# Moving a router's set-up arithmetic and one-hot tables from VectorE to GpSimd, and its blank output rows behind the set-up

## The chip, the cores and the metric

The kernel runs on one core of a Trainium2 chip. A core has TensorE (PE: matmuls and transposes), VectorE (DVE), ScalarE (ACT) and GpSimd (POOL), each of which takes its instructions in the order of the program, and SyncE (SP), whose queue starts most of the transfers, also in order. The engines wait for each other by semaphores. The metric is the device time of one execution in microseconds; lower is better.

## The reference

Three layers follow each other. Thresholded attention over 4 batches, 8 heads, 576 positions and 64 columns a head; then a mixture of 8 experts, of which each token takes the one with the largest logit; then a dense pair of layers over all 2304 tokens.

```python
scores = scale * np.matmul(q, k.transpose(0, 1, 3, 2))
thresh = np.max(scores, axis=-1, keepdims=True) - tau
scores = np.where(scores >= thresh, scores, -1e9)
attn = softmax(scores); x = attn @ v               # heads side by side: 2304 x 512
logits = x @ w_gate + modality_bias[modality_id]   # 2304 x 8
e_idx = np.argmax(logits, axis=1)
gate_w = softmax(logits)[np.arange(N), e_idx]
for e in range(E):                                 # 8 experts, 512 -> 1024 -> 512
    mask = e_idx == e
    y[mask] = gate_w[mask, None] * (np.maximum(x[mask] @ w1[e], 0) @ w2[e])
h = y @ w_in                                       # 512 -> 2048
return (h * sigmoid(1.702 * h)) @ w_out            # 2048 -> 512
```

## The kernel before

**Attention.** `Attention.run` goes through 72 iterations of two units; a unit is 128 rows of queries of one head against all keys, and nine units (`UPP`) make a pair of heads. TensorE computes the scores (`qk`, L234), VectorE takes the maximum (L245), ScalarE the exponential (L251), VectorE masks and sums (L275), TensorE transposes (L302) and multiplies by V (L348), ScalarE copies. GpSimd splits the next pairs' operands into high and low parts (`split`, L143 to L145; the last of the three buffers of `kA` and `kB` must be free for it) and scales finished rows (`row_items`, L386, L391), which SP writes to a buffer in DRAM, `x_dram` (L397).

**The side list.** Everything that doesn't belong to attention waits in a list, `side`. Each iteration takes one entry from it (`sides`; in the last 18 iterations up to eight, at five places). A `None` uses up a turn. At the start it holds seven `None`, then `gate_setup` (L102), the entries of `att.extra` (`blank_row` fills a tile on GpSimd, and ten `blank_rows` write it to the ten tiles of `y_rest` in DRAM, L1048 to L1052), and then the router's `setup_items`. Counted by iterations from 0, `gate_setup` is at 7, the blank rows at 8 to 18, and the set-up at 19 to 25. The order of instructions on each engine, and in SP's queue, is fixed by these lists when the program is built.

**The router.** `setup_items` (L543) loads the modality of each token (`mi`) and the biases (`bb`), makes row numbers and constants, and from them `idp` (the two digits of each token's number), `tri`, `rev`, `before`, `pages` and the bias of every token. After each batch `gate_items` finds the expert of each token. `assign` then gives every token a place in the experts' slots: assignment A after three batches (15 columns of 128 tokens, two slots), assignment B after the fourth (20 columns, all others). A token's place has two digits. `low` makes a one-hot table `OL` of the lower digit, 128 wide for each column of tokens, `high` one of the upper digit (`R`), `values` multiplies this by the token's number, and `sum_up` (L864) sums the products on TensorE; `lists` (L872 to L880) makes the indices for the gathers of it.

The order of these entries is at the end of `assign`:

```python
return [
    None, ranks, pages, starts, limits, slots, inside, counted, places, digits, high,
    lambda: (low(0, 5), values(0)), lambda: (low(5, 10), values(1)), lambda: low(10, n), gate,
    *[None] * (1 if first else NBW), lambda: sum_up(0, n), lists,
    ...
]
```

`gate`, behind the tables, ends with a copy on GpSimd (L670) and two writes by SP (L674) of each token's gate weight to `x_dram`.

**Experts and the last layer.** Seven slots of up to 512 tokens follow, two of assignment A and five of B. GpSimd gathers a slot's rows, TensorE transposes them (L929), and each slot takes eight steps of two matmul groups (L945, L967). SP loads an expert's weights in quarters (`ra` L1175, `rb` L1178); ScalarE rounds each (`ah`, `bh`, L1185) and VectorE takes the remainder (`al`, `bl`, L1186). Assignment B's arithmetic runs beside the steps of slot 0, and the weights of slot 1 are loaded behind it in SP's queue. Weights of the last layer are converted in between (L1089 to L1105). The last layer then runs over the tokens in blocks.

Of the kernel before, what the change touches and what calls it, by code (L numbers as in the profile page):

```python
# [14 lines left out]
ALU = mybir.AluOpType  # L15
# [6 lines left out]
NE = 8  # L22
# [3 lines left out]
PJ = 9  # L26
# [6 lines left out]
NS0 = 7  # L33
# [14 lines left out]
class Attention:  # L48
# [355 lines left out]
    def run(self):  # L404
        nc = self.nc
        NU = NPAIR * UPP
        self.load_first()
        self.load(1)
        rest = self.first()
        self.load_v(0)  # L410
        self.load_v(1)
        self.load(2)
        self.poolq = []
        self.avq, self.rowq, self.side = avq, rowq, side = [], [], []
        side += [None] * NS0 + [self.gate_setup, *self.extra] + self.router.setup_items(self.setup)
        it = done = 0
        while done < NU:
            last = it >= IT_LAST
            us = [u for u in (2 * it, 2 * it + 1) if u < NU]
            ts = [u for u in (2 * it - 2, 2 * it - 1) if 0 <= u < NU]  # L420
            starts = [u // UPP for u in us if u % UPP == 0]
            for p in starts:
                if p + 3 < NPAIR:
                    self.load(p + 3)
                if p + 2 < NPAIR:
                    self.load_v(p + 2)
                for n in range(1 if p == 0 else p + 2, min(p + 3, NPAIR)):
                    self.operands(n)
                    self.poolq += [lambda n=n, i=i: self.split(n, i, NPC) for i in range(NPC)]
            copies = []  # L430
            for i in range(2):
                if i < len(us):
                    self.qk(us[i])
                if i < len(ts):
                    copies += self.trans(ts[i])
                if i == 0 and not last:
                    n = AV1[it % 9]
                    while n and avq:
                        avq.pop(0)()
                        n -= 1  # L440
            for i in range(2):
                for c in range(2):
                    if CO[c] == 2 * i and c < len(copies):
                        copies[c]()
                if i < len(us):
                    self.max(us[i])
                    self.exp(us[i])
                for c in range(2):
                    if CO[c] == 2 * i + 1 and c < len(copies):
                        copies[c]()  # L450
                if last:
                    self.sides(SD[i], False)
            while rest:
                rest.pop(0)()
            for i, u in enumerate(us):
                self.mask(u)
                if last:
                    self.sides(SD[i + 2], False)
            n = AVL[it - IT_LAST] if last else AV[it % 9]
            while n and avq:  # L460
                avq.pop(0)()
                n -= 1
            for u in ts:
                self.trans_tails(u)
            n = ROWL[it - IT_LAST] if last else ROW[it % 9]
            while n and rowq:
                rowq.pop(0)()
                n -= 1
            n = 1
            while n and self.poolq:  # L470
                self.poolq.pop(0)()
                n -= 1
            self.sides(SD[4] if last else SN)
            for u in ts:
                done = u + 1
                p, w = divmod(u, UPP)
                if w == UPP - 1:
                    avq += self.av_items(p)
                    if p % 2:
                        avq.append(lambda b=p // HP, hh=p % HP // 2: rowq.extend(self.row_items(b, hh)))  # L480
            it += 1
# [33 lines left out]
PG = 512  # L515
# [7 lines left out]
class Router:  # L523
# [19 lines left out]
    def setup_items(self, tmp_pool):  # L543
        nc, c = self.nc, self.c
        T = lambda shape, name, dt=F32: c.tile(shape, dt, name=name)
        W = lambda shape, name, dt=F32: tmp_pool.tile(shape, dt, name=name)
        mi = W([64, B, PJ, 2], "mi", I32)
        bb = W([128, 2, NE], "bb")
        midf = W([128, B, 5], "midf")
        self.bias = T([128, NCOL, NE], "bias")  # L550
        tmp = W([128, NCOL, NE], "tmpb")
        nmid = W([128, NCOL], "nmid")
# [3 lines left out]
        pf = W([128, 1], "pf")  # L556
        ia = W([128, B, 5], "ia", I32)
        ib = W([128, B, 5], "ib", I32)
        i2 = W([128, 2, NCOL], "i2", I32)
# [12 lines left out]
        flat = midf.rearrange("p b c -> p (b c)")  # L572
        wide = lambda a: a.broadcast_to([128, NCOL, NE])
# [26 lines left out]
            nc.vector.tensor_scalar(i2[:, 1], iaf, 63, None, op0=ALU.bitwise_and)  # L600

        def tables():
            nc.vector.tensor_copy(self.idp, i2)
            nc.vector.tensor_scalar(self.tri, self.iota, pf[:, 0:1], None, op0=ALU.is_gt)
            nc.vector.tensor_scalar(self.rev, self.iota[:, 0:NE], -1.0, float(NE), op0=ALU.mult, op1=ALU.add)

        def order():
            e = self.iota[:, 0:NE]
            nc.vector.tensor_tensor(
                self.before, e.unsqueeze(2).broadcast_to([128, NE, NE]), e.unsqueeze(1).broadcast_to([128, NE, NE]),  # L610
                op=ALU.is_gt)
            nc.vector.tensor_scalar_mul(self.pages, e, float(PG))

        def modality():
            nc.vector.tensor_copy(midf[0:64], mi[:, :, 0:PJ:2, 0])
            nc.vector.tensor_copy(midf[64:128, :, 0:4], mi[:, :, 1:PJ:2, 0])
            nc.vector.tensor_scalar(nmid, flat, -1.0, 1.0, op0=ALU.mult, op1=ALU.add)

        def bias():
            nc.vector.tensor_mul(self.bias, wide(flat.unsqueeze(2)), wide(bb[:, 1:2, :]))  # L620
            nc.vector.tensor_mul(tmp, wide(nmid.unsqueeze(2)), wide(bb[:, 0:1, :]))
            nc.vector.tensor_add(self.bias, self.bias, tmp)

        return [loads, ids, parts, tables, order, modality, bias]

    def gate_items(self, b, lgt):
        nc, wk = self.nc, self.c
# [64 lines left out]
    def assign(self, ph, gate):  # L692
        nc, wk = self.nc, self.wk[ph]
        first = ph == "A"
# [9 lines left out]
        plf = T([128, 2, n], "plf")  # L704
        OL = T([128, n, 128], "OL", BF16)
# [136 lines left out]
            yield  # L842

        def low(c0, c1):
            nc.vector.tensor_tensor(
                OL[:, c0:c1], self.iota.unsqueeze(1).broadcast_to([128, c1 - c0, 128]),
                plf[:, 1, c0:c1].unsqueeze(2).broadcast_to([128, c1 - c0, 128]), op=ALU.is_equal,
            )

        def high():  # L850
            nc.vector.tensor_tensor(
# [2 lines left out]
            )  # L854

        def values(i):
            eng = nc.vector if i and first else nc.gpsimd
            eng.tensor_mul(R[:, :, i, :], R[:, :, 1, :], self.idp[:, i, 0:n].unsqueeze(2).broadcast_to([128, n, nh]))

        def sum_up(c0, c1):  # L860
# [24 lines left out]
        def compact():  # L885
# [12 lines left out]
# [4 lines that stand above are left out]
            *([] if first else [None] * 12 + [gaps, compact, None, bounds]),  # L902
# [578 lines left out]
```

## Time and profile before

| | |
|---|---|
| median of 3 runs | 985.03 us (983.91 to 985.19) |
| profiled execution | 986.93 us, span from first to last instruction 985.2 us |
| TensorE | 933.6 us busy (95%), granted clock 0.984 of full on average |
| VectorE | 556.5 us busy (56%) |
| ScalarE | 448.2 us busy (45%) |
| GpSimd | 236.2 us busy (24%) |

Attention takes the first 310 us or so, the experts run to about 600 us, the last layer to the end. The shares are averages over these stages, which have different limits; a stage has to be read by itself, from its own stretch of the timeline. A row of the timeline gives start, duration, engine, line and operation, and in square brackets how long the engine was idle before it and what it waited for. GpSimd's durations include time in which it waits for its port to the memory.

### The profile page before, as it was taken

The page shows a single profiled execution, that of the slowest core. Times are in us where ns is not written, and L with a number is a line of the kernel's source. Part 1 is how long each engine was busy: PE and PEld are TensorE (multiplying, and loading weights), DVE is VectorE, ACT ScalarE, POOL GpSimd, SP SyncE. Part 2 cuts the span into 40 slices and gives each one's busy share as a digit, 9 for nine tenths or more (in the row PEclk, how much of TensorE's full clock was granted, in tenths as well). Part 3 has the DMA queues.
Part 4 walks back from the last instruction along what each step waited for, and adds up shares of the span by engine and source line. Part 5 has one row for each costly group of instructions (what it writes and reads, how often), then busy time and mean ns, then how long its engine had stood idle before and what let it go on. Part 6 is the DMA issues. An engine that isn't in the chain of part 4 may idle for free. (4 is left out here: it accounts for less than half of the span.)

```text
span 985.2 us, 13988 instructions
## 1 busy us (share of the span) xinstructions
PE 933.6 (95%) x5009; PEld 751.8 (76%) x5009; DVE 556.5 (56%) x1194; ACT 448.2 (45%) x803; POOL 236.2 (24%) x322
## 2 busy tenths in 40 slices
PE   7899899999987989999999999999999999999994
PEld 6677777777764768777788888888888888888894
DVE  5888888888895487676776569961111111111110
ACT  4677687777774334444444435441222222222221
POOL 5935465476313332020212010010001000100100
PEclk7999999999999999999999999999999999999998
DMA  6776654755405336545545124320011000100100
GB/s 197 167 191 173 145 147 114 168 136 143 109 3 154 112 101 198 171 155 190 195 161 193 65 87 152 122 100 12 1 44 43 1 1 22 43 1 1 38 6 24
DMA packets 61308, 100.60 MB, mean 102 GB/s; under 512 B 9073, under 2 KB 32625, under 8 KB 61234
## 3 DMA queue, kind: packets, MB, share of 16 engines
q1 hardware_dynamic: 57394, 87.15, 30.4%
q0 software_dynamic: 3840, 12.50, 3.8%
q8 instruction: 42, 0.69, 0.3%
q14 instruction: 32, 0.26, 0.1%
HBM read 63.99 MB, written 17.23 MB: 82 GB/s over the span
## 5 line engine op out<-in xcount | busy, mean ns | idle before, releaser
L1161 DVE TENSOR_TENSOR hl<-sg,hh 128x512 fp32r<-128x512 f32 (+1 forms) x80 | 51.0, 638 | 243.1 <-ACT hh L1159 243.1
L1158 ACT ACTIVATE sg<-tr 128x512 f32<-128x512 f32 (+1 forms) x80 | 44.2, 553 | 208.6 <-PE tr L945 207.2
L245 DVE TENSOR_SCALAR_CACHE_REDUCE e<-sc,taue 128x576 f32<-128x576 f32 x144 | 116.3, 813 | 31.3 <-PE sc L234 27.3
L251 ACT ACTIVATE e<-e,thr 128x576 f32<-128x576 f32 x144 | 111.2, 776 | 31.1 <-DVE e L245 30.4
L234 PE MATMUL sc<-kA,qT 128*128 128x288 f32 x320 | 104.6, 343 | 20.9 <-DVE E L275 16.4
L945 PE MATMUL tr<-xh,wi_h 128*128 128x512 f32 (+1 forms) x320 | 120.7, 377 | 0.0
L945 PE MATMUL tr<-xh,wi_l 128*128 128x512 f32 (+1 forms) x320 | 118.9, 372 | 0.0
L945 PE MATMUL tr<-xl,wi_h 128*128 128x512 f32 (+1 forms) x320 | 118.8, 371 | 0.0
L967 PE MATMUL sc<-wo_h,hl 128*128 128x512 f32 x288 | 113.9, 395 | 0.0
L967 PE MATMUL sc<-wo_l,hh 128*128 128x512 f32 x288 | 113.8, 395 | 0.0
L967 PE MATMUL sc<-wo_h,hh 128*128 128x512 f32 x288 | 113.6, 395 | 0.0
L275 DVE SCALAR_TENSOR_TENSOR E<-sc,thr,e 128x576 f32<-128x576 f32 x128 | 103.5, 815 | 8.3 <-ACT e L251 4.6
L304 ACT COPY AT<-tr 128x512 f32<-128x512 f32 x128 | 73.8, 577 | 43.6 <-PE tr L302 43.5
L234 PE MATMUL sc<-kB,qT 128*128 128x288 f32 x320 | 91.3, 301 | 0.6 <-DVE kB L215 0.5
L234 PEld LDWEIGHTS sc<-kA,qT 128*128 128x128 f32 x320 | 61.9, 193 | 37.7 <-issue 22.0
L302 PE MATMUL tr<-ident,E 128*128 128x128 f32 x512 | 79.1, 278 | 0.0
L348 PE MATMUL av<-AT,V 128*64 128x288 f32 x512 | 77.4, 422 | 0.0
L945 PEld LDWEIGHTS tr<-xh,wi_l 128*128 128x128 f32 x320 | 60.3, 188 | 11.3
L945 PEld LDWEIGHTS tr<-xl,wi_h 128*128 128x128 f32 x320 | 60.4, 189 | 11.0
L945 PEld LDWEIGHTS tr<-xh,wi_h 128*128 128x128 f32 x320 | 60.3, 188 | 11.1
L967 PE MATMUL sc<-bl,hh 128*128 128x512 f32 x152 | 60.9, 401 | 5.1 <-DVE bl L1186 5.1
L945 PE MATMUL tr<-xl,ah 128*128 128x512 f32 (+1 forms) x160 | 61.7, 385 | 3.3 <-DVE xl L932 3.3
(215 smaller groups left out, 1753.4 us busy)
## 6 DMA issues: line engine op xcount, KB each, us to landing
ra<-in_moe_w_dram SPq DMA_DIRECT2D x20, 512.0 KB, 5.7
rb<-in_moe_w_dram SPq DMA_DIRECT2D x20, 512.0 KB, 4.1
F<-in_kq_dram SPq DMA_DIRECT2D x15, 640.0 KB, 4.8
cv_raw<-in_moe_w_in_dram SPq DMA_DIRECT2D x16, 512.0 KB, 5.3
cv_raw<-in_moe_w_out_dram SPq DMA_DIRECT2D x16, 512.0 KB, 3.6
V<-in_vp_dram SPq DMA_DIRECT2D x16, 320.0 KB, 4.7
kA<-kA SPq DMA_DIRECT2D x15, 320.0 KB, 3.5
kB<-kB SPq DMA_DIRECT2D x15, 320.0 KB, 3.5
```

Source lines behind the costliest of these rows:

```text
L234: nc.tensor.matmul(sc[:, hf, 0:288], l, d[kk][:, c0 + hf * 288:c0 + (hf + 1) * 288], start=(i == 0), stop=(i == len(ops) - 1),)
L245: nc.vector.tensor_scalar(e, d["sc", w][:, :, 0:288], self.taue[:, 0:1], 3.0e38, op0=ALU.add, op1=ALU.min, accum_out=thr)
L251: self.nc.scalar.activation(d["e", w], d["e", w], ACTF.Exp, bias=d["thr", w][:, 0:1], scale=-1.0)
L275: nc.vector.scalar_tensor_tensor(out=E.rearrange("p (a c) -> p a c", a=2), in0=d["sc", w][:, :, 0:288], scalar=d["thr", w][:, 0:1], in1=d[ ...
L302: nc.tensor.transpose(tp[:, kc * 128:(kc + 1) * 128], E[:, k0 + kc * 128:k0 + (kc + 1) * 128], self.ident)
L304: copies.append(lambda: nc.scalar.copy(AT[:, h, :, c * 128:(c + 1) * 128], tp.rearrange("p (k c) -> p k c", k=4)))
L348: nc.tensor.matmul(d["av"][h * 64:(h + 1) * 64, 0:288], d["V"][:, h, kc, :], d["AT"][:, h, kc, hf * 288:(hf + 1) * 288], start=False, stop ...
L945: nc.tensor.matmul(hps[:, 0:T], w[:, kd, :], blk[x][:, kd, :], start=(i == 0), stop=(i == 11))
L967: nc.tensor.matmul(y, h[:, cs], w, start=(f == 0 and i == 0), stop=(f == blk["nf"] - 1 and i == 2))
L1158: nc.scalar.activation(sg, hps, ACTF.Gelu_apprx_sigmoid)
L1161: return [upper, lambda: nc.vector.tensor_sub(hl, sg, hh.bitcast(F32))]
```

## The change

The router's set-up comes ahead of the blank rows in the side list, with one `None` between its second and third entry. By the count of iterations, the set-up moves from 19 to 25 to 8 to 15, and the blank rows from 8 to 18 to 16 to 26. Ten of the set-up's instructions go from VectorE to GpSimd: those of `tables`, `modality` and `bias`, and `pages`. The three of `parts` and `before` stay on VectorE.

In both assignments `low` is made by GpSimd, one instruction for each column of tokens (15 in A, 20 in B) that compares `iota` with one scalar per partition, where VectorE made five to ten columns in one instruction with both operands broadcast. `values(1)` of assignment A goes to GpSimd too; the other three products were there already.

```diff
--- before.py
+++ after.py
@@ -412,7 +412,7 @@
         self.load(2)
         self.poolq = []
         self.avq, self.rowq, self.side = avq, rowq, side = [], [], []
-        side += [None] * NS0 + [self.gate_setup, *self.extra] + self.router.setup_items(self.setup)
+        side += [None] * NS0 + [self.gate_setup, *self.router.setup_items(self.setup), *self.extra]
         it = done = 0
         while done < NU:
             last = it >= IT_LAST
@@ -600,28 +600,28 @@
             nc.vector.tensor_scalar(i2[:, 1], iaf, 63, None, op0=ALU.bitwise_and)
 
         def tables():
-            nc.vector.tensor_copy(self.idp, i2)
-            nc.vector.tensor_scalar(self.tri, self.iota, pf[:, 0:1], None, op0=ALU.is_gt)
-            nc.vector.tensor_scalar(self.rev, self.iota[:, 0:NE], -1.0, float(NE), op0=ALU.mult, op1=ALU.add)
+            nc.gpsimd.tensor_copy(self.idp, i2)
+            nc.gpsimd.tensor_scalar(self.tri, self.iota, pf[:, 0:1], None, op0=ALU.is_gt)
+            nc.gpsimd.tensor_scalar(self.rev, self.iota[:, 0:NE], -1.0, float(NE), op0=ALU.mult, op1=ALU.add)
 
         def order():
             e = self.iota[:, 0:NE]
             nc.vector.tensor_tensor(
                 self.before, e.unsqueeze(2).broadcast_to([128, NE, NE]), e.unsqueeze(1).broadcast_to([128, NE, NE]),
                 op=ALU.is_gt)
-            nc.vector.tensor_scalar_mul(self.pages, e, float(PG))
+            nc.gpsimd.tensor_scalar_mul(self.pages, e, float(PG))
 
         def modality():
-            nc.vector.tensor_copy(midf[0:64], mi[:, :, 0:PJ:2, 0])
-            nc.vector.tensor_copy(midf[64:128, :, 0:4], mi[:, :, 1:PJ:2, 0])
-            nc.vector.tensor_scalar(nmid, flat, -1.0, 1.0, op0=ALU.mult, op1=ALU.add)
+            nc.gpsimd.tensor_copy(midf[0:64], mi[:, :, 0:PJ:2, 0])
+            nc.gpsimd.tensor_copy(midf[64:128, :, 0:4], mi[:, :, 1:PJ:2, 0])
+            nc.gpsimd.tensor_scalar(nmid, flat, -1.0, 1.0, op0=ALU.mult, op1=ALU.add)
 
         def bias():
-            nc.vector.tensor_mul(self.bias, wide(flat.unsqueeze(2)), wide(bb[:, 1:2, :]))
-            nc.vector.tensor_mul(tmp, wide(nmid.unsqueeze(2)), wide(bb[:, 0:1, :]))
-            nc.vector.tensor_add(self.bias, self.bias, tmp)
-
-        return [loads, ids, parts, tables, order, modality, bias]
+            nc.gpsimd.tensor_mul(self.bias, wide(flat.unsqueeze(2)), wide(bb[:, 1:2, :]))
+            nc.gpsimd.tensor_mul(tmp, wide(nmid.unsqueeze(2)), wide(bb[:, 0:1, :]))
+            nc.gpsimd.tensor_add(self.bias, self.bias, tmp)
+
+        return [loads, ids, None, parts, tables, order, modality, bias]
 
     def gate_items(self, b, lgt):
         nc, wk = self.nc, self.c
@@ -842,10 +842,8 @@
             yield
 
         def low(c0, c1):
-            nc.vector.tensor_tensor(
-                OL[:, c0:c1], self.iota.unsqueeze(1).broadcast_to([128, c1 - c0, 128]),
-                plf[:, 1, c0:c1].unsqueeze(2).broadcast_to([128, c1 - c0, 128]), op=ALU.is_equal,
-            )
+            for c in range(c0, c1):
+                nc.gpsimd.tensor_scalar(OL[:, c], self.iota, plf[:, 1, c:c + 1], None, op0=ALU.is_equal)
 
         def high():
             nc.vector.tensor_tensor(
@@ -854,7 +852,7 @@
             )
 
         def values(i):
-            eng = nc.vector if i and first else nc.gpsimd
+            eng = nc.gpsimd
             eng.tensor_mul(R[:, :, i, :], R[:, :, 1, :], self.idp[:, i, 0:n].unsqueeze(2).broadcast_to([128, n, nh]))
 
         def sum_up(c0, c1):
```

## Rows read from the trace of the kernel before

**Rows 1.** Windows: start to end and length, busy us by engine, clock, DMA.
```profile
366.00:370.00 4.00, 4.00 (x15) 3.16 (x13) 2.02 (x4) 0.62 (x1) 0.00 (x0) 0.57 0.89 272
...
600.00:700.00 100.00, 100.00 (x442) 81.14 (x442) 60.84 (x106) 38.87 (x67) 4.76 (x8) 1.00 0.25 81
```

**Rows 2.** Timeline, VectorE (start, us, what): first maximum of iterations 18, 27, 36.
```profile
82.94 0.72 DVE L245 TENSOR_SCALAR_CACHE_REDUCE e<-sc,taue 128x576 f32<-128x576 f32 x1
...
122.31 0.72 DVE L245 TENSOR_SCALAR_CACHE_REDUCE e<-sc,taue 128x576 f32<-128x576 f32 x1
...
157.93 0.81 DVE L245 TENSOR_SCALAR_CACHE_REDUCE e<-sc,taue 128x576 f32<-128x576 f32 x1
```

**Rows 3.** Timeline at 102 us: GpSimd and VectorE.
```profile
102.40 1.56 POOL L145 TENSOR_TENSOR kB<-F,kA 128x640 fp32r<-128x640 f32 x1
...
102.44 1.56 DVE L603 CAST idp<-i 128x40 bf16<-128x40 int32 x1
```

**Rows 4.** Groups of GpSimd by line: count, busy us, mean ns, idle before.
```profile
L143 POOL TENSOR_SCALAR F<-F,cq 64x640 f32<-64x640 f32 x30 | 56.6, 1888 | 17.2 <-DMA F<-in_kq_dram 14.5
...
L144 POOL CAST kA<-F 128x640 fp32r<-128x640 f32 x30 | 21.4, 714 | 10.0 <-issue 6.4 <-PE sc L234 1.0 <-POOL F L143 0.8
...
L391 POOL TENSOR_TENSOR lgt<-xr,r 128x32 f32<-128x32 f32 x32 | 8.2, 256 | 0.0
...
L591 POOL CAST iota<-ii 128x128 f32<-128x128 int32 x1 | 0.3, 281 | 0.0
...
L592 POOL CAST pf<-pi 128x1 f32<-128x1 int32 x1 | 0.2, 178 | 0.0
```

**Rows 5.** Timeline of assignment A's tables: GpSimd, TensorE.
```profile
293.00 1.16 POOL L386 TENSOR_TENSOR xrow<-xr,r 128x256 f32<-128x256 f32 x1 [17.87 <-ACT xr L383]
...
294.89 0.82 POOL L391 TENSOR_TENSOR lgt<-xr,r 128x32 f32<-128x32 f32 x1
...
295.67 0.38 POOL L858 TENSOR_TENSOR R<-R,idp 128x120 bf16<-128x120 bf16 x1
...
299.26 0.61 POOL L386 TENSOR_TENSOR xrow<-xr,r 128x256 f32<-128x256 f32 x1
...
300.81 0.53 PE L864 MATMUL tr<-R,OL 128*128 128x16 bf16 x15
```

**Rows 6.** Timeline of assignment B's tables: VectorE, GpSimd, TensorE.
```profile
355.87 1.16 DVE L851 TENSOR_TENSOR R<-iota,plf 128x960 bf16<-128x960 f32 x1
...
357.11 2.31 POOL L858 TENSOR_TENSOR R<-R,idp 128x960 bf16<-128x960 bf16 x1 [9.68 <-DVE R L851]
...
357.68 2.42 DVE L845 TENSOR_TENSOR OL<-iota,plf 128x640 bf16<-128x640 f32 x1
...
359.49 2.26 POOL L858 TENSOR_TENSOR R<-R,idp 128x960 bf16<-128x960 bf16 x1
...
363.70 0.25 POOL L670 COPY g<-g 128x80 f32<-128x80 f32 x1 [1.95 <-DVE g L668]
...
364.12 1.22 DVE L1186 TENSOR_TENSOR bl<-rb,bh 128x1024 fp32r<-128x1024 f32 x1
...
365.39 0.50 PE L967 MATMUL sc<-bl,hh 128*128 128x512 f32 x1 [2.60 <-DVE bl L1186]
...
366.17 0.69 DVE L1092 SCALAR_TENSOR_TENSOR cv_a<-cv_raw,cv_a 128x512 int32<-128x512 int32 x1
```

**Rows 7.** Timeline behind assignment B: SP's queue, ScalarE, VectorE, TensorE.
```profile
363.98 1.29 SPq L674 DMA_DIRECT2D x_dram<-g  x2
...
365.48 0.44 SPq L1175 DMA_DIRECT2D ra<-in_moe_w_dram  x1
...
369.38 1.05 ACT L1185 CAST ah<-ra 128x1024 fp32r<-128x1024 f32 x1 [6.18 <-DMA ra<-in_moe_w_dram]
...
376.71 1.22 DVE L1186 TENSOR_TENSOR bl<-rb,bh 128x1024 fp32r<-128x1024 f32 x1
...
379.62 0.39 PE L967 MATMUL sc<-bl,hh 128*128 128x512 f32 x1
```

## The prediction

> **What bounds the kernel now.** I read the windows first. From 600 us on TensorE has no gap, in a stretch where VectorE is busy for 61 of 100 us [rows 1]: nothing there can be won by freeing VectorE, and whatever the kernel gains or loses before that is carried to the end unchanged. So three places count, those that the change edits: the set-up at 98 to 118 us, the tables of assignment A at 292 to 301 us, and those of assignment B at 355 to 380 us.
>
> In the attention loop I read the start of the first maximum of every ninth iteration, because the loop's extra work repeats with period nine. Iterations 27 to 35 took 35.62 us (122.31 to 157.93). Iterations 18 to 26, which hold the set-up arithmetic, took 39.37 [rows 2]. The reader sees 3.75 us that the set-up costs in a loop where the next scores wait for VectorE's masks. One part of it is a lock: the CAST to `idp`, 40 columns, took 1.56 us, exactly while GpSimd's product at 102.40 ran [rows 3].
>
> In stage B the timeline shows the wait that the change aims at: VectorE makes the table until 363 us, `bl` follows at 364.12, and TensorE stands still for 2.60 us until 365.39 [rows 6]. Then its granted clock is 0.57 in the next 4 us [rows 1], 1.2 GHz for most of them, which costs another 4 x 0.43 = 1.7 us. So some 4.3 us meet the eye here. But the same stage has a second chain, in SP's queue, and it decides the forecast.
>
> **The price of one column.** The change makes 35 one-column compares on GpSimd (15 in A, 20 in B), 128x128 f32 to bf16, against a scalar of the partition. The trace has no such instruction. The nearest is L143, GpSimd's TENSOR_SCALAR with a scalar per partition: 1888 ns for 640 columns [rows 4]. Taken in proportion that is 0.38 us for 128 columns. Taken with the fixed part that a one-column CAST shows (178 ns), it is 0.18 + 128 x 1.71/640 = 0.52. Consecutive instructions start some 0.04 us before the last one ends (294.89 + 0.82 against 295.67, [rows 5]), so a column takes 0.34 to 0.48 of the queue. From below the bound is the 128-column CAST, 281 ns, so 0.24. I take c = 0.41, the middle of the two readings of L143, which is the same operation; the CAST is another.
>
> A page speaks against this. The Trainium skill, GPSIMD Engine Reference, section 4.1, says that GpSimd is about half as fast as VectorE with two inputs but runs at roughly line rate with one. L143 has one tensor input and does not agree: 2.9 ns a column, where the CAST of 128 columns took 281 ns in all. By the page's rule a column would cost no more than that CAST, and the sum below would come out at -1.7 us in place of +5.1.
>
> **Set-up.** Ten small VectorE instructions leave the loop, `idp` with its lock among them; `parts` (three) and `before` (one) stay. Of the 3.75 us I leave 0.6 for these four, an estimate, and count -3.15 us. On GpSimd the ten cost between 0.18 us (one column) and 0.61 (a 256-column product, [rows 5]) each, 2 to 6 us together over five iterations. What hides them is that GpSimd runs ahead of VectorE here: the split that follows waits 6.4 us for its operand buffers (L144, [rows 4]). The set-up loads `mi` and `bb` now stand before the load of a later pair in SP's queue; that pair's split stands in that same wait. The ten blank rows go out some eight iterations later, onto transfers that nothing in the loop waits for; the rows written into their place come much later. I cost these moves at nothing; without the cover it is the third rival.
>
> **Assignment A.** VectorE loses three pieces of the table and a product. On GpSimd, `low` and `values` stand behind two pairs of products that before were stretched by VectorE's table pieces: 1.16 against 0.61, and 0.82 against the usual 0.26 [rows 4, 5]. Without these the queue comes free at 295.67 - 0.55 - 0.56 = 294.56. The tables then end at 294.56 + 15c + 2 x 0.38 = 295.32 + 15c, which is 301.5 for c = 0.41. The summing matmuls that need them ran at 300.81. TensorE takes its work in order: scores, transposes and `av` of the iteration are queued behind them, ScalarE's copies and VectorE's masks wait for those. So A gives 15c - 5.49 = +0.66 us. The freed VectorE time doesn't help, since it only brings TensorE to this wait sooner. The four gathers that follow hang on the same lists and move with them.
>
> **Assignment B.** What is late next is `g`. Its copy stands on GpSimd behind all of the table (363.70 before), and SP writes it out at 363.98 ahead of the next expert's weights: `ra` at 365.48, which ScalarE had waited 6.18 us for at 369.38, and so on through VectorE's conversions to `bl` at 376.71 to 377.93 [rows 6, 7]. From the copy to the end of this `bl` are 14.23 us, nearly all of it back-to-back; TensorE used the result at 379.62, so the slack is 1.69 us. If the copy starts after 365.39, TensorE is later than before, stall at 365.39 or not.
>
> When does it start? GpSimd has the digits at 355.87, when VectorE starts `high`. The products `values` take 1.65 us each: the second shows 2.26, but VectorE's table piece, started at 357.68 and blocked by the first product, held the port until 360.10, and the product was done at 361.75 [rows 6]. The same rows show how the two engines share: one instruction of one runs, then one of the other. So GpSimd also loses `high` (1.16) and four VectorE instructions that come along meanwhile, `bl` to the third step of a weight conversion, 364.12 to 366.86 before, 2.74 us. The copy starts at 355.87 + 1.16 + 3.30 + 2.74 + 20c = 363.07 + 20c: 371.3 for c = 0.41. B gives 363.07 + 20c - 365.39 = 20c - 2.32 = +5.9 us. The 4.3 us of stall and low clock at 365 go, but TensorE gets to the next expert's first matmuls 4 us sooner only to wait longer for their weights: ScalarE and VectorE hold the remaining conversions behind the same load.
>
> **Sum.** -3.15 + (15c - 5.49) + (20c - 2.32) = 35c - 10.96 = +3.4 us at c = 0.41. Both new standstills (about 3 us in A, some 6 in B) can be followed by a stretch at the lower clock, 0 to 1.7 us each by [rows 1]; half of both is 1.7. That is +5.1 us. On the profiled execution, 986.93 us with a span of 985.2, it makes 992.0; that run was 1.9 above the median of the timed ones, so I put it on the median: 985.03 + 5.1 = 990.1. At c = 0.34 it is +2.6 (987.6), at c = 0.48 +7.5 (992.5), and 994.2 with both clock stretches whole. About 2 us (0.2%) is what a measurement of this kernel tells from no change.
>
> **Rivals.**
> The cheap column (chance 0.17), the other side: a compare costs what a CAST does, c = 0.24. A gives -1.9, B +2.5, the sum is -2.56, and with half a clock stretch in B -1.7: 983.3. It decides below c = 0.27, where 35c - 10.96 + 1.7 changes its sign. For it: all other one-input instructions on GpSimd in rows 4. Against: L143, 30 instances of the very operation. This is how it would go by the Trainium skill's rule of one input (GPSIMD Engine Reference, section 4.1).
>
> No lost turns (0.11): GpSimd's compares are so short that VectorE's instructions slip between them and cost it nothing; 1.16 + 2.74 = 3.9 us come off B: 986.2. Against it stand the stretched products of rows 5.
>
> The set-up gives nothing back (0.11): GpSimd reaches `ids` or the tables later than VectorE needs them, or the later blank rows hold up the row writes, on which GpSimd waits for its buffers. Then 3.15 us are missing: 993.3. For it: VectorE did wait for GpSimd's `ib` before.
>
> **How the numbers follow.** The forecast (c from 0.34 to 0.48, SP's chain behind `g`) has 0.61; its own range is 987 to 994. The range 982.5 to 995 takes in the cheap column below and the lost set-up gain above. Faster than 983.1: half of the cheap column and the least of the others, 0.15. Within 2 us: the rest of it, most of no lost turns, and the forecast's lowest end, 0.20. Slower: 0.65.
>
> **What would show it.** Right: a `low` column of 0.38 to 0.52 us on GpSimd; iterations 18 to 26 near 36 us; the summing matmuls of A after 301; no wait of TensorE on `bl` near 365, but SP's writes of `g` near 371 and TensorE idle from about 372 to 378, ended by the weights. Wrong: columns under 0.3 us, or `ra` issued by SP without waiting for `g`.

## The result, and the profile after

The changed kernel takes 996.62 us (median of 4 runs, 995.47 to 998.63) where the kernel before took 984.84 in the runs beside it: ratio 1.0122, 95% interval 1.0096 to 1.0148. The profiled execution took 997.37 us with a span of 995.5, so 10.3 us more span than before. The direction is the forecast's, the size is not: +11.8 us on the median against +5.1, and the time lies 1.6 us above the upper end of the range. (Lines behind 846 carry numbers two lower than before.)

The groups of GpSimd instructions by line (count, busy us, mean ns, idle before), the kernel after:
```profile
L846 POOL TENSOR_SCALAR OL<-iota,plf 128x128 bf16<-128x128 f32 x35 | 23.1, 676 | 8.5 <-DVE plf L841 8.5
...
L604 POOL TENSOR_SCALAR tri<-iota,pf 128x128 bf16<-128x128 f32 x1 | 0.6, 618 | 0.0
L603 POOL CAST idp<-i 128x40 bf16<-128x40 int32 x1 | 0.2, 216 | 6.8 <-DVE i L600 6.8
```
The column of 128, which the kernel before did not have, is L846: 676 ns in the mean, 618 where nothing disturbs it (L604 is the same form). The CAST to `idp` costs 0.22 us in place of the 1.56 of [rows 3].

The timeline of the kernel after (start, us, what; idle before and what ended it):
```profile
82.77 0.72 DVE L245 TENSOR_SCALAR_CACHE_REDUCE e<-sc,taue 128x576 f32<-128x576 f32 x1
...
118.35 0.72 DVE L245 TENSOR_SCALAR_CACHE_REDUCE e<-sc,taue 128x576 f32<-128x576 f32 x1
...
297.16 2.91 POOL L846 TENSOR_SCALAR OL<-iota,plf 128x128 bf16<-128x128 f32 x5
...
297.24 0.40 PE L862 MATMUL tr<-R,OL 128*128 128x16 bf16 x10 [1.83 <-POOL R L856]
...
300.13 0.20 PE L862 MATMUL tr<-R,OL 128*128 128x16 bf16 x1 [0.38 <-POOL OL L846]
...
300.29 1.27 SPq L674 DMA_DIRECT2D x_dram<-g  x2
...
303.83 1.27 POOL L1009 DMA_INDIRECT xg<-x_dram,igaA  x1 [2.02 <-DMA x_dram<-g]
...
325.49 0.50 PE L943 MATMUL tr<-xh,ah 128*128 128x512 f32 x1
...
357.06 5.58 POOL L846 TENSOR_SCALAR OL<-iota,plf 128x128 bf16<-128x128 f32 x5 [8.52 <-DVE plf L841]
...
369.04 5.79 POOL L846 TENSOR_SCALAR OL<-iota,plf 128x128 bf16<-128x128 f32 x10
374.79 0.25 POOL L670 COPY g<-g 128x80 f32<-128x80 f32 x1
375.06 1.29 SPq L674 DMA_DIRECT2D x_dram<-g  x2
376.56 0.44 SPq L1173 DMA_DIRECT2D ra<-in_moe_w_dram  x1
380.46 1.04 ACT L1183 CAST ah<-ra 128x1024 fp32r<-128x1024 f32 x1 [16.14 <-DMA ra<-in_moe_w_dram]
381.56 0.79 PE L943 MATMUL tr<-xh,ah 128*128 128x512 f32 x1 [6.45 <-ACT ah L1183]
387.80 1.22 DVE L1184 TENSOR_TENSOR bl<-rb,bh 128x1024 fp32r<-128x1024 f32 x1
389.07 0.50 PE L965 MATMUL sc<-bl,hh 128*128 128x512 f32 x1 [0.76 <-DVE bl L1184]
```
and its windows (length, busy us by engine, clock, DMA):
```profile
300.00:304.00 4.00, 3.87 (x14) 2.26 (x15) 2.04 (x8) 0.76 (x2) 1.98 (x7) 0.50 0.22 42
...
376.00:382.00 6.00, 0.44 (x1) 0.44 (x2) 0.46 (x1) 1.54 (x2) 0.00 (x0) 0.57 0.78 244
382.00:386.00 4.00, 3.96 (x10) 2.54 (x9) 3.86 (x8) 2.62 (x5) 0.00 (x0) 0.50 0.54 174
```
The timeline of the kernel before, around assignment A:
```profile
299.33 1.26 SPq L674 DMA_DIRECT2D x_dram<-g  x2
...
302.92 1.25 POOL L1011 DMA_INDIRECT xg<-x_dram,igaA  x1 [2.08 <-DVE igaA L880]
...
323.76 0.50 PE L945 MATMUL tr<-xh,ah 128*128 128x512 f32 x1
```
The 10.3 us can be read off by stage, each time against the row of before:

- Set-up: iterations 18 to 26 take 35.58 us (82.77 to 118.35) for 39.37 [rows 2]: -3.8.
- Assignment A: the summing matmuls (L862) wait for columns, one by one, to 300.13. SP writes `g`, whose copy on GpSimd also stands behind the columns, at 300.29 in place of 299.33, so +1.0 where the set-up had brought 3.8: A costs 4.8. The first of the gathers waits for just this write (303.83, after 2.02 us, ended by `x_dram<-g`); before, the indices `igaA` released it at 302.92. TensorE's clock is at 0.50 from 300 to 304. The first expert's matmul is at 325.49 for 323.76, which is 0.7 more. One pair of traces doesn't price this last stretch: from the end of the sum to that matmul it took 25.2 us after the change and 22.4 before, but 18.6 with the set-up part alone (the first experiment).
- Assignment B: the matmul that needs `bl` is at 389.07 for 379.62 [rows 7], so +9.5, 7.7 of it since 325.49. TensorE waits 6.45 us for the weights, at a clock of 0.57, and is at 0.50 for the next 4 us.
- From there to the end: 606.4 us for 605.6, +0.8. The last layer took 461.7 us in both, from the first load of `y_first` (533.78 and 523.45) to the end, so this lies ahead of it.

### The profile page after: what moved, and what is told of

It is laid out like the page before. It is cut to its first block, busy times and chain, and to the rows that moved or that the text cites. A ratio compares the mean times of both kernels' runs of the same rounds, so it can differ in the third digit from the quotient of the medians.

```text
span 995.5 us, 14025 instructions
## 1 busy us (share of the span) xinstructions
PE 938.1 (94%) x5009; PEld 751.8 (76%) x5009; DVE 545.4 (55%) x1177; ACT 448.2 (45%) x803; POOL 259.2 (26%) x368
## 5 line engine op out<-in xcount | busy, mean ns | idle before, releaser
L943 PE MATMUL tr<-xh,ah 128*128 128x512 f32 (+1 forms) x160 | 64.4, 403 | 6.4 <-ACT ah L1183 6.4
L943 PEld LDWEIGHTS tr<-xl,wi_h 128*128 128x128 f32 x320 | 60.3, 188 | 11.1
```

Source lines behind the costliest of these rows:

```text
L943: nc.tensor.matmul(hps[:, 0:T], w[:, kd, :], blk[x][:, kd, :], start=(i == 0), stop=(i == 11))
```

## The experiments

Two theories stood at the start. One: the forecast's mechanism with a dearer column; all 35 columns stand on the path, 15 ahead of A's sum, 20 ahead of SP's write of `g` in B. Two: something else costs (the freed VectorE or the moved queues) and the column's price is incidental.

**Parts: the set-up alone.** VectorE makes both tables as before; only the set-up arithmetic, its place and the blank rows are changed.

> Only the set-up part of the change: set-up on GpSimd and ahead of the blank rows, the tables of both assignments on VectorE as before. By my theory the set-up gives 3.8 us and all of the loss is in the tables: 981.0. Rival, the later blank rows and GpSimd's set-up cost something later on: 983 to 986.

Measured: 980.92 us, ratio 0.996 (0.9934 to 0.9986). The set-up part is a gain, about the one foretold. Its trace has the first gather of assignment A released by `igaA`, and still the stall of 2.6 us:
```profile
299.07 1.26 POOL L1011 DMA_INDIRECT xg<-x_dram,igaA  x1 [2.09 <-DVE igaA L880]
...
357.56 0.50 PE L967 MATMUL sc<-bl,hh 128*128 128x512 f32 x1 [2.59 <-DVE bl L1186]
...
394.90 0.50 PE L967 MATMUL sc<-bl,hh 128*128 128x512 f32 x1 [2.21 <-DVE bl L1186]
```
Here the clock doesn't fall behind the stall, as it did before (0.57, [rows 1]):
```profile
360.00:365.00 5.00, 5.00 (x25) 4.10 (x24) 2.55 (x5) 2.06 (x3) 0.00 (x0) 1.00 1.07 366
```

**Parts: the set-up and B.** A's tables go back to VectorE:
```diff
         def low(c0, c1):
+            if first:
+                nc.vector.tensor_tensor(OL[:, c0:c1], ...)
+                return
             for c in range(c0, c1):
...
-            eng = nc.gpsimd
+            eng = nc.vector if i and first else nc.gpsimd
```


> The change, but assignment A's tables are made by VectorE as before; B's stay on GpSimd. It splits the loss. By my theory A costs 5 us (a wait of the summing matmuls and the low clock behind it) and B 9 to 10: 991. Rival, the two wait for the same thing, so that A's delay is hidden in B's: 995 to 997.

Measured: 992.62 us, ratio 1.0076 (1.0055 to 1.0098); 11.7 us above the set-up alone on the same chip. B alone makes the kernel slow. TensorE's wait and the copy of `g` that sets it stand in its trace:
```profile
365.34 0.25 POOL L670 COPY g<-g 128x80 f32<-128x80 f32 x1
...
372.13 0.80 PE L949 MATMUL tr<-xh,ah 128*128 128x512 f32 x1 [6.47 <-ACT ah L1189]
```

**Parts: the set-up and A.** The other half: `if not first` in the same place, both products on GpSimd.

> The set-up part of the change and assignment A's tables on GpSimd (15 columns and both products), assignment B's columns on VectorE as before. Theory (A's 15 columns stand ahead of the sum that TensorE's queue waits for: in the change's trace SP wrote A's g at 300.29 us, with the set-up part alone at 295.47, so 4.8 us, and TensorE's clock falls behind the standstill): 980.9 + 4.8 + 0.7 = 986.4 us, range 984.5 to 988.5; it is then the time of the change less B's 20 columns (11.7 us: 984.9). Rival (A's price is the prediction's term, 15c - 5.49 with the measured c of 0.58, so 3.2 us, or less since the tail of the attention waits for the first expert's weights anyway): 981 to 984.

Measured: 985.86 us beside 983.18 of the kernel before on that chip, ratio 1.0017 (0.9996 to 1.0038). Over the ratio of the set-up alone that is 0.0057, 5.6 us, the theory's size; but its interval of some 3.3 us either way takes in the 3.2 of the bare columns too. The trace decides for the theory, and names what comes on top, the gathers' wait for `g`:
```profile
301.79 0.20 PE L868 MATMUL tr<-R,OL 128*128 128x16 bf16 x1 [0.38 <-POOL OL L852]
...
305.49 1.27 POOL L1015 DMA_INDIRECT xg<-x_dram,igaA  x1 [2.02 <-DMA x_dram<-g]
```
Iteration 18 starts 1.57 us later here than with the set-up alone (84.42 for 82.85). Less this, the sum ends 2.9 us later (301.99 for 297.48) and the first gather starts 4.85 us later (305.49 for 299.07). The clock falls meanwhile:
```profile
299.00:302.00 3.00, 1.29 (x17) 0.82 (x17) 0.00 (x0) 0.00 (x0) 3.00 (x7) 0.51 0.00 0
302.00:306.00 4.00, 4.00 (x15) 2.40 (x16) 2.04 (x8) 0.76 (x2) 1.98 (x5) 0.51 0.26 51
```
From 302 to 306 TensorE is busy throughout at half speed, which is 2 us of work at full speed. But 3.5 of these 4 us lie ahead of the first gather, which waits for `g` and not for TensorE, so that the clock adds to the time is not shown. The parts, -0.4%, +0.6% and +1.1%, give the whole, +1.2%, within their intervals.

**The chain behind `g`.** The whole change with one entry of the list moved, the gate (the copy of `g` and SP's rows) ahead of B's tables:
```diff
-            None, ..., digits, high,
+            None, ..., digits, *([] if first else [gate]), high,
...
-            lambda: low(10, n), gate,
+            lambda: low(10, n), *([gate] if first else []),
```


> The change, but in assignment B the entry that makes and writes g stands ahead of the tables. By my theory B's loss is that SP's queue holds the next expert's weights behind g, and g behind the columns: SP issues g near 359 and ra right behind; TensorE then waits only for the last column (near 375) and starts the next expert's first matmuls near 376 in place of 381.6; some 11 us come back at the end of that wait, 986. Rival, the table itself is late for its summing matmuls and TensorE waits for it, or VectorE is slowed by the shared port: 994 to 997.

Measured: 988.48 us, ratio 1.0034 (1.001 to 1.0058): 8 of the 12 us are gone, the rest not. SP issues `ra` at 357.06, and the wait for weights is gone, as the theory says. What it left out is the second consumer, the sum:
```profile
355.56 1.29 SPq L674 DMA_DIRECT2D x_dram<-g  x2
357.06 0.44 SPq L1173 DMA_DIRECT2D ra<-in_moe_w_dram  x1
...
371.41 0.22 PE L862 MATMUL tr<-R,OL 128*128 128x96 bf16 x1 [1.22 <-POOL OL L846]
...
377.60 0.26 PE L862 MATMUL tr<-R,OL 128*128 128x96 bf16 x1 [0.32 <-POOL OL L846]
377.70 0.77 PE L943 MATMUL tr<-xh,ah 128*128 128x512 f32 x1
```
The columns now run beside VectorE's weight conversions and take 0.80 us each in the mean of all 35, for 0.68. They end at 377.5, and TensorE's queue stands before them.

**The dose.** Each column made twice:
```diff
             for c in range(c0, c1):
-                nc.gpsimd.tensor_scalar(OL[:, c], ...)
+                for _ in range(2):
+                    nc.gpsimd.tensor_scalar(OL[:, c], ...)
```


> The whole change, with each of GpSimd's 35 columns made twice, the second time over the first (the same values). Theory (all 35 columns stand one behind the other on the path, 0.58 us each): 996.6 + 35 x 0.58 = 996.6 + 20.3 = 1016.9 us, range 1015 to 1022 (TensorE stands longer, so its clock may fall longer); in the trace the copy of g ends 20 us later than in the change's. Rival (the columns were mostly covered, and what cost was one place: the clock after the standstill, or the wait ahead of the sum): the second 35 lie beside other work in the same measure, and the time rises by less than 10 us, to 1006 at most.

Measured: 1019.23 us, ratio 1.0337 (1.0311 to 1.0364). 35 more columns cost 22.6 us over the change's median, above the theory's 20.3. A column of a pair took longer, ten of them 6.41 us, 0.64 each; two of 0.64 for one of 0.58 are 0.70 more, and 24.5 us for 35. Nearly all of it arrives in the time, so the cost grows with the columns, as the theory says. SP's second write of `g` stands 22 us later than after the change:
```profile
305.19 6.41 POOL L847 TENSOR_SCALAR OL<-iota,plf 128x128 bf16<-128x128 f32 x10
...
311.82 1.27 SPq L674 DMA_DIRECT2D x_dram<-g  x2
...
397.01 1.29 SPq L674 DMA_DIRECT2D x_dram<-g  x2
```

**The price of a column by itself.** Forty GpSimd instructions of several forms, writing into tables that nothing reads any more, put into the set-up-only kernel; first at the start of the last layer's second block:

> The disputed price by itself: forty GpSimd instructions of ten forms, four of each, stand in the second block of the last layer, where GpSimd has little else to do (they write into tables that are no longer read). Tables are made by VectorE here, set-up as changed. If the price is that of this instruction (a compare of 128 f32 columns with one scalar per partition), it shows about 0.62 us alone as it did in the tables; if the tables' price was raised by VectorE's use of the shared port, it shows 0.3 to 0.5 alone. If it is the scalar per partition that costs, the same compare with an immediate shows about 0.3, as the CAST; if it is the compare, the product with a scalar per partition shows less than the compare; if it is a loop over columns, 64 and 16 columns show about 0.40 and 0.25.

Inconclusive: 980.69 us, but VectorE converts weights there (569 to 609 us), and all forms came out stretched, the compare at 819 ns in the mean, the plain cast at 527. So once more in the third block, where VectorE is nearly idle:

> The set-up part alone, with 40 GpSimd instructions at the start of the last layer's third block, where VectorE converts no weights; they write tables that nothing reads any more: in fours, 128 f32 columns to bf16 compared with, and multiplied by, a value per partition, compared with a constant, bf16 to bf16, 64 columns, 16 columns, a plain cast, and three f32 forms in place. Theory (a start of some 0.2 us and about 3 ns an element): 128 columns 0.58 to 0.62, 64 columns 0.40, 16 columns 0.25, the cast 0.28, with no difference between constant and per-partition value. Rival (the value per partition makes the price): 0.58 with it, 0.28 to 0.3 with a constant. The time is that of the set-up part alone.

Measured: 977.12 us, one run. The groups of GpSimd's instructions by line and form:
```profile
L1364 POOL TENSOR_SCALAR tri<-iota,place 128x128 bf16<-128x128 f32 x8 | 5.0, 628 | 0.7
L1364 POOL TENSOR_SCALAR tri<-iota 128x128 bf16<-128x128 f32 x4 | 2.1, 528 | 0.3
L1364 POOL TENSOR_SCALAR tri<-iota,place 128x64 bf16<-128x64 f32 x4 | 1.8, 442 | 0.4
L1379 POOL CAST tri<-iota 128x128 bf16<-128x128 f32 x4 | 1.6, 394 | 0.3
L1364 POOL TENSOR_SCALAR tri<-iota,place 128x16 bf16<-128x16 f32 x4 | 1.3, 321 | 0.4
```
16 columns take 321 ns and 128 take 628: 2.7 ns a column and a fixed 0.28 us. A constant in place of the value per partition saves 0.1 of 0.63, so the scalar's kind is a small part of the price. The cast came out dearer than expected (0.39).

**A 16-bit row.** The whole change, with the row that the columns compare held in bf16:
```diff
-        self.iota = T([128, 128], "iota")
+        self.iota, self.iotab = T([128, 48], "iota"), T([128, 128], "iotab", BF16)
```


> The whole change, with the row 0 to 127 that the columns compare held in bf16 (exact), so that a GpSimd column reads 16 bits and writes 16. Theory (a GpSimd column has a price of its own per element, whatever the width): 0.58 us a column and the time of the change, 995 to 998. Rival (the 32-bit input sets the price, as the CAST of 128 columns at 0.28 us could say): about 0.4 us a column, and by 35 columns on the path 996.6 - 35 x 0.18 = 990.3 us.

Measured: 989.59 us, ratio 1.0052 (1.003 to 1.0075). That is the rival's number, and yet the rival is wrong: the column costs what it did, and all stages up to the last layer are as late as after the change (its first load at 533.76 and 533.78). The gain lies in the last layer, 454.4 us to the end of the span for 461.7, where nothing was edited. Groups of TensorE by line from 660 to 900 us, after the change and here, and GpSimd's column here:
```profile
L965 PE MATMUL sc<-wo_h,hl 128*128 128x512 f32 x168 | 66.4, 395 | 0.0
```
```profile
L847 POOL TENSOR_SCALAR OL<-iotab,plf 128x128 bf16<-128x128 bf16 x35 | 23.1, 677 | 8.5 <-DVE plf L842 8.5
...
L966 PE MATMUL sc<-wo_h,hl 128*128 128x512 f32 x172 | 67.0, 390 | 0.0
```
The same matmuls take 390 ns in the mean for 395. The two rows together are 64 bytes shorter than the one was, so by the sizes every later tile lies 64 bytes lower. Two kernels ask whether that is it. One gives the f32 row 64 columns, which puts the addresses back:

> The run with the 16-bit row again, but the f32 row that stays beside it has 64 columns in place of 48, so that the two take 512 bytes of a partition, as the one row did in the change, and each later tile lies where it lay there. The run with the 16-bit row was 7.4 us shorter than the change in the last layer alone (from the first load of y_first to the end 454.4 us against 461.7), where nothing of it was edited. Theory (the last layer is shorter because its tiles moved by 64 bytes): with the addresses back the last layer takes 461.7 again, and the time is the change's, 995 to 998. Rival (something else of that kernel or that run made it short): 454.4 again and 989.6.

Measured: 997.12 us, ratio 1.0111 (1.0084 to 1.0138), the matmul at 395 ns again, 461.8 us from the first load of `y_first` (535.28) to the end (997.1). The only edit between the two runs is the length of that row, so the place of the later tiles makes it, and 16 bits change nothing about the column. The other applies the shift to the next version below.

**Versions that could beat both.** First, B's columns on GpSimd but off the path: set-up as changed, A on VectorE (the edit of "The set-up and B"), the gate ahead (the edit of "The chain behind `g`"), and the sum three entries later.
```diff
...
-NBW = 6
+NBW = 9
...
```


> The set-up part of the change, assignment A's tables on VectorE as before, assignment B's 20 columns on GpSimd but with the gate's entry (g, the rows of x_dram) ahead of them in the list, and the sum over the tables three None entries later (9 for 6). Theory (the columns cost only by what waits for them: SP behind g, and TensorE's sum): nothing on the path waits for a column any more, and the 2.59 us stall at bl that the kernel with the set-up part alone keeps goes, with the slow stretch of TensorE's clock behind it: 980.9 - 2.6 - 1.7 = 976.6 us, range 975 to 979. Rival (20 columns beside VectorE's conversions cost VectorE its turns, so that al and bl come late): the columns ran at 0.80 us in place of 0.58 there, so VectorE loses up to 20 x 0.58 = 11.6 us of turns in three steps of 6 us, and the time is that of the set-up part alone or more, 981 to 986.

Measured: 982.25 us, ratio 0.9979 (0.9965 to 0.9993): the rival's end. TensorE doesn't wait for `bl` at 357 any more, and still the kernel is no faster than the set-up alone. The columns are not quite off the path, and the next wait on `bl` stays:
```profile
373.97 0.22 PE L868 MATMUL tr<-R,OL 128*128 128x96 bf16 x1 [0.36 <-POOL OL L852]
...
393.88 0.79 PE L971 MATMUL sc<-bl,hh 128*128 128x512 f32 x1 [1.88 <-DVE bl L1190]
```
Behind it the clock is at 0.80 from 395 to 400 us. Whether turns that VectorE loses to the columns, the rival's reason, cost anything was not separated from this. Second, VectorE keeps the tables, in pieces spread over the steps:
```diff
...
+            None, ..., digits, gate, high, (low(0, 5), values(0)), None, (low(5, 10), values(1)),
+            None, low(10, 15), None, low(15, n), *[None] * (NBW - 3), sum_up(0, n), ...
...
```


> The set-up part of the change, all columns on VectorE; in assignment B the gate's entry stands ahead of the tables, and the four pieces of five columns are spread over the None entries ahead of the sum, which stays where it was. Theory (what the tables of B cost in the kernel before is the one stall of 2.6 us where they stand together, and the clock behind it): 980.9 - 2.6 - 1.7 = 976.6 us, range 975 to 979, with no engine changed. Rival (VectorE is full in these steps, and each piece of 5 columns puts off al or bl by its own length wherever it stands): 981, as the set-up part alone.

Measured: 979.16 us, ratio 0.9946 (0.9925 to 0.9967), 1.8 us under the set-up alone where 4.3 were expected, with intervals that overlap. Of the 4.3, 1.7 were for a slow clock behind the stall, and the trace of the set-up alone has none there. The stall goes from 2.59 to 0.52 us, but the next one stays, and here the clock falls behind it, which it did not in the set-up-only run:
```profile
358.16 0.50 PE L969 MATMUL sc<-bl,hh 128*128 128x512 f32 x1 [0.52 <-DVE bl L1188]
...
395.06 0.50 PE L969 MATMUL sc<-bl,hh 128*128 128x512 f32 x1 [1.83 <-DVE bl L1188]
```
```profile
395.00:400.00 5.00, 4.94 (x17) 3.96 (x18) 4.05 (x7) 0.43 (x2) 0.00 (x0) 0.66 0.72 242
```
So part of what is won at 357 is given back at 395: 5 x 0.34 = 1.7 us there. Last, the same version with every tile 64 bytes lower:

> The run with VectorE's pieces spread out (979.2 us), with the 16-bit row beside a 48-column f32 one, so that each later tile lies 64 bytes lower. Theory (the addresses make the last layer 7.4 us shorter): 979.2 - 7.4 = 971.8 us, range 969 to 975. Rival (no effect of addresses): 979.

Measured: 971.78 us, ratio 0.9863 (0.9833 to 0.9893), 1.4% faster than the kernel before, and the step of 7.4 us that was foretold. The last layer takes 454.5 us in it (512.62 to 967.1) for 461.9 without the shift (514.83 to 976.7).

## Why the prediction was right in direction and wrong in size

**The failed step is the price of one column.** The text took c = 0.41 from L143 (0.34 to 0.48) and 0.52 us as the longest reading of a duration. Measured were 0.62 alone, so 0.58 of the queue (five columns in 2.91 us). Thirty-five times the 0.17 that was missing is 6.0 us; with it the sum is 11.1, where 10.3 (span) and 11.8 (median) were measured. That it comes so near is in part luck, as the stages below show. The error sits in the fixed part. I took 0.18 us for it, from a one-column CAST, and in one of the two readings none at all; the forms run alone show 0.28 for this operation. Two rows of one operation, 640 columns at 1.89 us and 128 at 0.62, give 0.30 + 2.5 ns a column; one row can't separate the two. The Trainium skill's rule of line rate with one input (GPSIMD Engine Reference, section 4.1) disagrees with this trace more than the forecast did: 0.62 us for 128 columns, where the prediction priced the rule at no more than the CAST's 0.28.

**Set-up: right.** -3.8 us for -3.15, the lock on `idp` gone; the part alone measured -0.4%. The rival in which it gives nothing fell. The cover was read too firmly: of the 10.0 us that GpSimd stood idle before L144 [rows 4], the 6.4 are put down to "issue", time without a wait that the profile shows, and only 1.0 to TensorE's use of the operands.

**Assignment A: right place, too small, and one wait left out.** The sum waited for columns, as foretold, but at 300.1 instead of 301.5, since the set-up's gain is in front of it. The term 15c - 5.49 gives 3.2 at c = 0.58, and the end of the sum agrees (2.9 later with A alone). But 4.8 to 5.6 were measured in all. The prediction let the four gathers hang on the lists alone; they read the rows that hold `g`, and waited for its write, 2.02 us ended by `x_dram<-g`. Behind the first two gathers GpSimd makes the last rows of attention, and behind these SP issues the first expert's weights: at 308.92, for 304.15 with the set-up alone, which is 4.8 us again. So the chain behind `g`, which the prediction saw in B, stands in A too.

**Assignment B: the time right by two errors that cancel, the price too high.** The formula 363.07 + 20c gives 374.7 for the copy of `g`; it stands at 374.79. In it, GpSimd's start is 1.2 us later than assumed (357.06), and VectorE takes fewer turns: the first five columns took 5.58 us for 2.92 undisturbed, 2.66 us lost where I had 3.9. The rival without lost turns fell, though a third of the way toward it was right. So B itself cost 7.7 us from the first expert's matmul on, where 20c - 2.32 is 9.3; against the set-up alone, whose trace has the same stall and no slow clock behind it, the medians give 11.7. From the copy to the end of the `bl` that follows (387.80 + 1.22) are 14.23 us, the number of [rows 7] to the digit, so SP's chain behind `g` is as described; the run with the gate ahead shows it directly.

**The clock: came, its cost not shown.** The sum has 1.7 us for half of two slow stretches. Both came, at 0.50 from 300 to 304 us and from 382 to 386. But the first lies almost whole ahead of the first gather, which waits for `g`, and behind the second TensorE waits again, 0.76 us for the `bl` of 389.07. What either costs, no run shows.

**The cheap column** fell with c. That VectorE's relief is worth little here fits the run from the other side: without the stall at 357, and with two waits of 0.36 us left for columns, the kernel was no faster than the set-up alone.

## What to carry to other kernels

Before work goes to another engine, take that operation's cost from two sizes, so that fixed part and slope come apart, above all where one wide instruction becomes many narrow ones: here the fixed 0.28 us, 35 times, was 9.8 of 20.3 us. Then list everything that stands in a queue behind the new work, not only who reads its result: in both assignments it was SP's write of `g`, with the gathers waiting for it in A and the next expert's weights behind it in B. And time the parts of a bundled change alone; here one part won 4 us, and the other two lost 16.

## What the runs showed that was not expected

**64 bytes.** With every later tile 64 bytes lower in its partition, a 128x512 matmul of the last layer took 390 ns for 395 in the records, and the last layer 454.4 us for 461.7. With the addresses back it took 461.8; applied to another version it gave 7.4 us once more. Which tile's place it is, and why, was not tried.

**The clock after short waits.** In A, after the change, TensorE was busy for 1.2 of 4 us (296 to 300), and then for nearly 4 us at a granted clock of 0.50, which is 1.2 GHz. But equal waits don't always end so: the stall of 2.6 us on `bl` was followed by 0.57 before the change and by 1.00 with the set-up alone, and waits of about 2 us near 395 us by 0.66 in one run and by 1.00 in another. That can make runs of one kernel differ by a us or two for each such wait; that it does is not shown.
